# First chunk of x transposed by five DMA transposes, with w1's first slices on ScalarE's queue

## The chip, the cores and the metric

The kernel runs on one core of a Trainium2 chip. The metric is device time in microseconds (us), lower is better. TensorE is written PE in the profile (its weight loads PEld), VectorE DVE, ScalarE ACT, GpSimd POOL and SyncE SP.

## What is computed

The forward and backward pass of a small dense layer, all in bfloat16, with S = 2048 rows of x, D = 640 and F = 1536:

```python
def _fwd_reference(x, w1, w2):          # x [1, S, D], w1 [D, F], w2 [F, D]
    h = jnp.einsum("bsd,df->bsf", x, w1)
    h = jax.nn.silu(h)
    return jnp.einsum("bsf,fd->bsd", h, w2)

def reference(x, w1, w2, grad_out):
    out, vjp = jax.vjp(_fwd_reference, x, w1, w2)
    return (out, *vjp(grad_out))        # out, grad of x, of w1, of w2
```

## The kernel before

The rows of x are worked in four chunks of 512 (`SC`). In each chunk TensorE forms h transposed (F on the partitions, twelve tiles of 128, called `ft`; five steps `dt_` of 128 over D), ScalarE applies silu (`silu_a`, giving aT) and tanh for the derivative (`silu_grad`), then TensorE multiplies aT by w2 for the output (`sd_phase`), forms the gradient of the activation (`g_group`) and multiplies it by w1 transposed for the gradient of x (`sd_phase` again). The activations and their gradients are also stored to scratch in DRAM. After the four chunks the two weight gradients are formed from transposed reloads of that scratch. The h matmuls stand at L206, the gradient ones at L253, those of both `sd_phase` calls at L269, the weight gradients at L357 and L406 (the last tile at L387).

Matmuls contract over the partitions, so x must stand transposed in `xT` (D on the partitions). For chunks 1 to 3 `load_xT` does that with one DMA transpose each (L157). For chunk 0 the kernel loads x plainly in two halves (`x_two`, L173), transposes them on TensorE in twenty 128x128 pieces (L197, with an identity made on GpSimd), and copies the results from PSUM to `xT` on VectorE and ScalarE in turn (L199).

All other transfers are issued by SP, in the order in which they stand in its queue: the two halves of x, the first third of w1 (columns 0 to 511, `FC` = 512) in three pieces by rows (block 0, blocks 1 to `KM`-1, the rest; L178), the second and third thirds of w1 (L169), w2 (L186), then transposes of the first chunk of grad_out (`goT`, L162), of w2 in three pieces (`w2T`, L189) and of w1 (`w1T`, L190).

The start of the kernel has two special parts. 22 matmuls on a constant tile (`NWARM`, L145) keep TensorE at work from the start. And `start_before_entry_wait` moves the instructions listed in `early` (the constant tile's memset, those 22 matmuls, both x loads and the first pieces of w1), with all that stands before them on the same engine, ahead of the wait at which the engines meet on entry.

The first chunk's h is formed by `h_first`: for the first `KM` = 2 blocks of D it goes through four `ft` tiles per block, so that work can begin before all blocks are there; then it completes those four tiles and goes on tile by tile. The tanh of a tile follows its silu by up to `LAG_G` = 4 tiles. The eight PSUM buffers of `ps_h` are shared by all these stages. Transfers are tracked by eight semaphores in turn: the ninth transfer waits until the first has landed, and so on. The order of instructions within an engine is otherwise set by a scheduler.

Of the kernel before, what the change touches and what calls it, by code (L numbers as in the profile page):

```python
# [8 lines left out]

ACT = mybir.ActivationFunctionType  # L10
ALU = mybir.AluOpType
# [4 lines left out]
def start_before_entry_wait(nc, names):  # L16

    def move(nc):
        blocks = nc.m.functions[0].blocks
        entry, home = blocks[0].instructions, blocks[1].instructions
        for engine in {i.engine for i in home if i.name in names}:
            mine = [i for i in home if i.engine == engine]
            last = max(k for k, i in enumerate(mine) if i.name in names)
            moved = mine[: last + 1]
            gate = next(
                k
                for k, i in enumerate(entry)  # L30
                if i.engine == engine and isinstance(i, mybir.InstEventSemaphore)
            )
            taken = {i.name for i in moved}
            for k in reversed(range(len(home))):
                if home[k].name in taken:
                    del home[k]
            for i in reversed(moved):
                entry.insert(gate, i)

    nc.at_finalize(move)  # L40
# [22 lines left out]
def kernel(  # L63
# [11 lines left out]
    nc = tc.nc  # L75
    P = 128
    x2 = x.flatten_outer_dims()
# [5 lines left out]
    S, D = x2.shape  # L83
    F = w1.shape[1]
    ST, DT, FT = S // P, D // P, F // P
    SC = 512
    NCH = S // SC
    STC = SC // P
    FC = 512
# [1 line left out]
    FB = FC // P  # L91
    LAG = 2
    LAG_G = 4
    KM = 2
    NWARM = 22
    dt_in = x.dtype

# [3 lines left out]
    ps_h = ctx.enter_context(tc.tile_pool(name="ps_h", bufs=8, space=bass.MemoryType.PSUM))  # L101
# [10 lines left out]
    w1_v = w1.rearrange("(dt p) f -> p dt f", p=P)  # L112
# [19 lines left out]
    with ExitStack() as mctx:  # L132
        cpool = mctx.enter_context(tc.tile_pool(name="cpool", bufs=1))
# [7 lines left out]
        early = [nc.vector.memset(warm[:], 1.0)]  # L141
# [2 lines left out]
        for i in range(NWARM):  # L144
            early.append(nc.tensor.matmul(wp[:, 0:P], lhsT=warm[:], rhs=warm[:], start=True, stop=True))  # L145

        ident = cpool.tile([P, P], dt_in, name="ident")
        make_identity(nc, ident[:])

        w1_nat = w1pool.tile([P, DT, F], dt_in, name="w1_nat", tag="w1a")  # L150
        w2T = wpool.tile([P, DT, F], dt_in, name="w2T")
        w2_nat = wpool.tile([P, FT, D], dt_in, name="w2_nat")
# [2 lines left out]
        def load_xT(c):  # L155
            xT = xpool.tile([P, DT, SC], dt_in, name="xT")
            nc.sync.dma_start_transpose(out=xT[:], in_=x2[c * SC:(c + 1) * SC, :])  # L157
            return xT
# [4 lines left out]
            return goT  # L163

        xT_next = xpool.tile([P, DT, SC], dt_in, name="xT")
        x_two = cpool.tile([P, 2, 2, D], dt_in, name="x_two")

        def load_w1(lo, hi):
            nc.sync.dma_start(out=w1_nat[:, :, lo:hi], in_=w1_v[:, :, lo:hi])  # L169

        def load_x_half(half):
            lo = half * 2 * P
            return nc.sync.dma_start(  # L173
                out=x_two[:, half, :, :], in_=x2[lo:lo + 2 * P, :].rearrange("(p q) d -> p q d", q=2)
            )

        def load_w1_rows(lo, hi):
            return nc.sync.dma_start(out=w1_nat[:, lo:hi, 0:FC], in_=w1_v[:, lo:hi, 0:FC])  # L178

        early += [load_x_half(0), load_x_half(1), load_w1_rows(0, 1), load_w1_rows(1, KM)]  # L180
        load_w1_rows(KM, DT)
        start_before_entry_wait(nc, {i.ins.name for i in early})
        for fc in range(1, NFC):
            load_w1(fc * FC, (fc + 1) * FC)
# [3 lines left out]
        for fc in range(NFC):  # L188
            nc.sync.dma_start_transpose(out=w2T[:, :, fc * FC:(fc + 1) * FC], in_=w2[fc * FC:(fc + 1) * FC, :])  # L189
        nc.sync.dma_start_transpose(out=w1T[:], in_=w1[:, :])  # L190

        def pe_x_half(xT, half):
            lo = half * 2 * P
            for dt_ in range(DT):
                tp = ps_h.tile([P, 2, P], dt_in, name="tp", tag="hp")
                for q in range(2):
                    nc.tensor.transpose(tp[:, q, :], x_two[:, half, q, dt_ * P:(dt_ + 1) * P], ident[:])  # L197
                copy = nc.scalar.copy if dt_ % 2 else nc.vector.tensor_copy
                copy(out=xT[:, dt_, lo:lo + 2 * P].rearrange("p (s q) -> p q s", q=2), in_=tp[:])  # L199

        pe_x_half(xT_next, 0)
        pe_x_half(xT_next, 1)

        def h_mm(hp, ft, xT, lo, hi):
            for dt_ in range(lo, hi):
                nc.tensor.matmul(  # L206
                    hp[:],
                    lhsT=w1_nat[:, dt_, ft * P:(ft + 1) * P],
                    rhs=xT[:, dt_, :],
                    start=(dt_ == 0),  # L210
                    stop=(dt_ == DT - 1),
                )
# [19 lines left out]
        def h_first(xT, aT, ghT):  # L232
            hps = []
            for ft in range(FB):
                hps.append(ps_h.tile([P, SC], FP32, name="hp"))
            for dt_ in range(KM):
                for ft in range(FB):
                    h_mm(hps[ft], ft, xT, dt_, dt_ + 1)
            for i in range(FT + LAG_G):
                if i < FT:  # L240
                    if i < FB:
                        h_mm(hps[i], i, xT, KM, DT)
                    else:
# [40 lines left out]
        for c in range(NCH):  # L284
            xT, goT = xT_next, goT_next
# [3 lines left out]
            if c + 1 < NCH:  # L289
                xT_next = load_xT(c + 1)  # L290
# [8 lines left out]
            if c == 0:  # L299
                h_first(xT, aT, ghT)  # L300
                nc.sync.dma_start(
                    out=aT_scr[:, c * SC:(c + 1) * SC].rearrange("(ft p) s -> p ft s", p=P), in_=aT[:]
                )
                sd_phase(c, w2_nat, aT, oT_scr)
                for ft in range(FT):
                    g_group(ft, goT, ghT)
                nc.sync.dma_start(
                    out=ghT_scr[:, c * SC:(c + 1) * SC].rearrange("(ft p) s -> p ft s", p=P), in_=ghT[:]
# [4 lines left out]
            for i in range(FT + LAG):  # L313
# [7 lines left out]
                out=aT_scr[:, c * SC:(c + 1) * SC].rearrange("(ft p) s -> p ft s", p=P), in_=aT[:]  # L321
            )
            nc.sync.dma_start(
                out=ghT_scr[:, c * SC:(c + 1) * SC].rearrange("(ft p) s -> p ft s", p=P), in_=ghT[:]
# [7 lines left out]
    with ExitStack() as fctx:  # L332
# [17 lines left out]
        k = 0  # L350
# [26 lines left out]
        k = 0  # L377
        for fc in range(NFC):
            gh_blk = gh_blks[fc]
            for dt_ in range(DT):  # L380
                if dt_ == DT // 2:
                    store_gw2(fc)
                if fc == NFC - 1 and dt_ == DT - 1:
                    for k, (lo, hi) in enumerate(((0, FC - P), (FC - P, FC))):
# [12 lines left out]
                        else:  # L397
                            nc.vector.tensor_copy(out=g1[:, lo:hi], in_=gp[:, lo:hi])  # L398
                        last_store = nc.sync.dma_start(
                            out=gw1_v[:, dt_, fc * FC + lo:fc * FC + hi], in_=g1[:, lo:hi]  # L400
# [49 lines left out]
```

## Time and profile before

| | |
|---|---|
| median of 7 runs | 320.74 us (320.51 to 321.18) |
| profiled execution | 321.41 us, of which the span from first to last instruction is 319.5 us |
| first matmul of the warm-up | starts 0.50 us |
| first h matmuls | from 5.26 us on (in the chain of waits from 5.46) |
| first chunk's output matmuls | from 18.77 us on (in the chain from 18.94) |
| x by halves, 320 KB each | issued 0.09 and 0.54, landed 3.0 and 3.4 us later |
| table load on ScalarE | 0.73 to 2.01 us |
| first silu on ScalarE | 8.40 us |
| goT transpose's issue on SP | 4.75 to 16.0 us |

All times count from the first instruction of the span. The chain of waits is followed back from the last instruction: at each step to what released it, or to the instruction before it on its engine; work in it sets the end, other work does not. A transfer has two times: that for which its issue holds the engine, and that from issue to landing. A row of the timeline gives start, length, engine, line, operation and tiles; "x22" is how many instructions are merged in it. In rows by window, the engines' busy times stand in the order PE, PEld, DVE, ACT, POOL, then the granted clock, the DMA engines' busy share and GB/s.

### The profile page before, as it was taken

How to read it: one execution, taken by the hardware profiler on the slowest of the kernel's cores; microseconds unless marked ns; L12 is line 12 of the kernel's file. 1: busy time of each engine (PE TensorE's matmuls, PEld its weight loads, DVE VectorE, ACT ScalarE, POOL GpSimd, SP SyncE). 2: the span in 40 equal slices, each digit the busy share in tenths (PEclk: the TensorE clock that was granted, in tenths of full speed). 3: DMA queues.
4: the chain of work that ended last, by engine and by line, in shares of the span. 5: the costliest groups of instructions: out<-in, count | busy, mean ns of one | idle time of the engine just before them, and what ended most of it. 6: DMA issues, size and time to landing. Idle time of an engine off the chain costs nothing.

```text
span 319.5 us, 3570 instructions
## 1 busy us (share of the span) xinstructions
PE 316.2 (99%) x1498; PEld 146.3 (46%) x1498; DVE 102.6 (32%) x182; ACT 77.9 (24%) x142; POOL 0.7 (0%) x6
## 2 busy tenths in 40 slices
PE   9999999999999999999999999999999999999996
PEld 6444444444444444444444444444444444444443
DVE  3771541477510087710147741000000100001001
ACT  4960000545201254411054520110100001001100
POOL 0000000000000000000000000000000000000000
PEclk9999999999999999999999999999999999999999
DMA  8999999999999855292635079819999998996011
GB/s 280 322 208 222 215 309 240 342 256 289 277 284 282 207 188 163 84 310 75 161 119 140 2 258 268 216 23 296 261 213 253 261 244 297 235 297 220 33 37 45
DMA packets 147311, 67.33 MB, mean 211 GB/s; under 512 B 112608, under 2 KB 147040, under 8 KB 147296
## 3 DMA queue, kind: packets, MB, share of 16 engines
q1 hardware_dynamic: 147296, 67.12, 80.8%
q8 instruction: 11, 0.18, 0.2%
q14 instruction: 4, 0.03, 0.0%
HBM read 9.83 MB, written 28.97 MB: 121 GB/s over the span
## 4 chain that ended last, share of the span: by engine, by line
PE 98%; DMA 1%; DVE 0%; issue 0%; DVEq 0%; SPq 0%
PE hp L269 32%; PE hp L206 16%; PE hp L253 16%; PE hp L357 16%; PE hp L406 15%; PE hp L387 1%; DMA x_two<-in_x_dram 1%; PE tp L197 1%; DVE g L398 0%; DVEq L398 0%; SPq L434 0%
## 5 line engine op out<-in xcount | busy, mean ns | idle before, releaser
L206 PE MATMUL hp<-xT,w_nat 128*128 128x512 bf16 x240 | 57.4, 382 | 0.0
L253 PE MATMUL hp<-goT,w2T 128*128 128x512 bf16 x240 | 56.9, 379 | 0.0
L269 PE MATMUL hp<-aT,w_nat 128*128 128x512 bf16 x240 | 52.5, 379 | 0.0
L269 PE MATMUL hp<-ghT,w1T 128*128 128x512 bf16 x240 | 52.5, 379 | 0.0
L357 PE MATMUL hp<-a_blk,go_nat 128*128 128x512 bf16 x240 | 52.0, 379 | 0.0
L406 PE MATMUL hp<-gh_blk,x_nat 128*128 128x512 bf16 x224 | 48.5, 379 | 0.0
L277 ACT ACTIVATE oT<-hp 128x512 bf16<-128x512 f32 x24 | 14.3, 597 | 109.8 <-PE hp L269 109.8
L215 ACT ACTIVATE aT<-hp 128x512 bf16<-128x512 f32 x48 | 30.0, 627 | 33.1 <-PE hp L206 33.1
L206 PEld LDWEIGHTS <-w_nat 128*128 128x128 bf16 x240 | 23.7, 99 | 28.5 <-issue 0.8
L357 PEld LDWEIGHTS <-go_nat 128*128 128x128 bf16 x240 | 23.5, 98 | 28.3
L253 PEld LDWEIGHTS <-w2T 128*128 128x128 bf16 x240 | 23.5, 98 | 28.3
L269 PEld LDWEIGHTS <-w1T 128*128 128x128 bf16 x240 | 23.5, 98 | 28.3
L269 PEld LDWEIGHTS <-w_nat 128*128 128x128 bf16 x240 | 23.5, 98 | 28.3
L279 DVE CAST oT<-hp 128x512 bf16<-128x512 f32 x16 | 11.1, 692 | 77.0 <-PE hp L269 77.0
L260 DVE SCALAR_TENSOR_TENSOR ghT<-ghT,hp 128x512 bf16<-128x512 bf16 x48 | 32.5, 682 | 7.3 <-PE hp L253 7.3
L406 PEld LDWEIGHTS <-x_nat 128*128 128x128 bf16 x224 | 21.9, 98 | 26.4
L222 DVE SCALAR_TENSOR_TENSOR ghT<-aT,v 128x512 bf16<-128x512 bf16 x48 | 32.8, 687 | 0.5
L221 DVE TENSOR_SCALAR v<-t 128x512 bf16<-128x512 f32 x48 | 20.3, 426 | 30.6 <-ACT t L219 30.6
L219 ACT ACTIVATE t<-hp 128x512 f32<-128x512 f32 x48 | 29.9, 628 | 0.0
L417 DVE CAST g<-hp 128x512 bf16<-128x512 f32 x7 | 4.8, 692 | 47.0 <-PE hp L406 27.8
L367 DVE CAST g2T<-hp 128x512 bf16<-128x512 f32 x7 | 4.8, 691 | 46.1 <-PE hp L357 46.1
L365 ACT ACTIVATE g2T<-hp 128x512 bf16<-128x512 f32 x8 | 4.8, 597 | 47.0 <-PE hp L357 47.0
(20 smaller groups left out, 27.0 us busy)
## 6 DMA issues: line engine op xcount, KB each, us to landing
aT_scr<-aT SPq DMA_DIRECT2D x4, 1536.0 KB, 6.2
ghT_scr<-ghT SPq DMA_DIRECT2D x4, 1536.0 KB, 8.0
out_dram<-o_sb SPq DMA_DIRECT2D x8, 640.0 KB, 3.6
oT_scr<-oT SPq DMA_DIRECT2D x4, 640.0 KB, 3.6
go_nat<-in_grad_out_dram SPq DMA_DIRECT2D x4, 640.0 KB, 6.6
x_nat<-in_x_dram SPq DMA_DIRECT2D x4, 640.0 KB, 5.4
gxT_scr<-oT SPq DMA_DIRECT2D x4, 640.0 KB, 4.7
w_nat<-in_w_dram SPq DMA_DIRECT2D x1, 1920.0 KB, 12.3
```

Source lines behind the costliest of these rows:

```text
L206: nc.tensor.matmul(hp[:], lhsT=w1_nat[:, dt_, ft * P:(ft + 1) * P], rhs=xT[:, dt_, :], start=(dt_ == 0), stop=(dt_ == DT - 1),)
L215: nc.scalar.activation(aT[:, ft, :], hp[:], ACT.Silu)
L219: nc.scalar.activation(t[:], hp[:], ACT.Tanh, scale=0.5)
L221: nc.vector.tensor_scalar(out=v[:], in0=t[:], scalar1=-0.5, scalar2=0.5, op0=ALU.mult, op1=ALU.add)
L222: nc.vector.scalar_tensor_tensor(out=ghT[:, ft, :], in0=aT[:, ft, :], scalar=1.0, in1=v[:], op0=ALU.subtract, op1=ALU.mult)
L253: nc.tensor.matmul(gp[:], lhsT=w2T[:, dt_, ft * P:(ft + 1) * P], rhs=goT[:, dt_, :], start=(dt_ == 0), stop=(dt_ == DT - 1),)
L260: nc.vector.scalar_tensor_tensor(out=ghT[:, ft, :], in0=ghT[:, ft, :], scalar=1.0, in1=gp[:], op0=ALU.add, op1=ALU.mult)
L269: nc.tensor.matmul(op_[:], lhsT=w_all[:, ft, dt_ * P:(dt_ + 1) * P], rhs=rhs_all[:, ft, :], start=(ft == 0), stop=(ft == FT - 1),)
L277: nc.scalar.activation(oT[:, dt_, :], op_[:], ACT.Copy)
L279: nc.vector.tensor_copy(out=oT[:, dt_, :], in_=op_[:])
L357: nc.tensor.matmul(gp[:], lhsT=go_nat[:, st, dt_ * P:(dt_ + 1) * P], rhs=a_blk[:, st, :], start=(st == 0), stop=(st == ST - 1),)
L406: nc.tensor.matmul(gp[:], lhsT=x_nat[:, st, dt_ * P:(dt_ + 1) * P], rhs=gh_blk[:, st, :], start=(st == 0), stop=(st == ST - 1),)
```

## The change

The first chunk of x is no longer loaded plainly and transposed on TensorE. Five DMA transposes on SP, one for each 128 columns of x (512 rows each), write `xT` directly, ahead of the entry wait. The first third of w1 is loaded by ScalarE's queue, in three pieces (block 0, block 1, blocks 2 to 4), all of them ahead of the entry wait. `KM` becomes 3. The identity, `x_two`, the TensorE transposes and their copies are gone. The other loads keep their place in SP's queue.

```diff
-    KM = 2
+    KM = 3
...
-        ident = cpool.tile([P, P], dt_in, name="ident")
-        make_identity(nc, ident[:])
...
-        x_two = cpool.tile([P, 2, 2, D], dt_in, name="x_two")
...
-        def load_x_half(half):
-            lo = half * 2 * P
-            return nc.sync.dma_start(
-                out=x_two[:, half, :, :], in_=x2[lo:lo + 2 * P, :].rearrange("(p q) d -> p q d", q=2)
-            )
-
         def load_w1_rows(lo, hi):
-            return nc.sync.dma_start(out=w1_nat[:, lo:hi, 0:FC], in_=w1_v[:, lo:hi, 0:FC])
-
-        early += [load_x_half(0), load_x_half(1), load_w1_rows(0, 1), load_w1_rows(1, KM)]
-        load_w1_rows(KM, DT)
+            return nc.scalar.dma_start(out=w1_nat[:, lo:hi, 0:FC], in_=w1_v[:, lo:hi, 0:FC])
+
+        for k in range(DT):
+            early.append(
+                nc.sync.dma_start_transpose(out=xT_next[:, k, :], in_=x2[0:SC, k * P:(k + 1) * P])
+            )
+        early += [load_w1_rows(0, 1), load_w1_rows(1, 2), load_w1_rows(2, DT)]
         start_before_entry_wait(nc, {i.ins.name for i in early})
...
-        def pe_x_half(xT, half):
-            lo = half * 2 * P
-            for dt_ in range(DT):
-                tp = ps_h.tile([P, 2, P], dt_in, name="tp", tag="hp")
-                for q in range(2):
-                    nc.tensor.transpose(tp[:, q, :], x_two[:, half, q, dt_ * P:(dt_ + 1) * P], ident[:])
-                copy = nc.scalar.copy if dt_ % 2 else nc.vector.tensor_copy
-                copy(out=xT[:, dt_, lo:lo + 2 * P].rearrange("p (s q) -> p q s", q=2), in_=tp[:])
-
-        pe_x_half(xT_next, 0)
-        pe_x_half(xT_next, 1)
```

## The prediction

> **What bounds the kernel now.** I read the page first, for the busy shares and the chain; then the chain in order of time; then the timeline of the first 24 us; and last the DMA rows that come nearest to what is added.
>
> ```profile
> span 319.5 us, 3570 instructions
> PE 316.2 (99%) x1498; PEld 146.3 (46%) x1498; DVE 102.6 (32%) x182; ACT 77.9 (24%) x142; POOL 0.7 (0%) x6
> PE 98%; DMA 1%; DVE 0%; issue 0%; DVEq 0%; SPq 0%
> ```
>
> TensorE is busy for 99% of the span and makes 98% of the chain. Only its opening can be shortened: from about 5 us on, no other engine or transfer is in the chain until the last store.
>
> ```profile
> 0.09 3.01 DMA x_two<-in_x_dram
> 3.15 2.31 PE tp L197 x20
> 5.46 13.47 PE hp L206 x60
> 18.94 12.95 PE hp L269 x60
> ```
>
> These rows of the chain in order of time give start, length and work. The first half of x lands at 3.10; twenty transposes run to 5.46; then come the 60 matmuls of the first chunk's h and the 60 of its output. Both groups of 60 are 128x512, yet one takes 13.47 us and the other 12.95 (216 ns each): 0.52 us is lost inside the first group. The timeline shows where:
>
> ```profile
> 0.50 2.53 PE L145 MATMUL wp<-warm 128*128 128x128 bf16 x22 [0.50 <-DVE warm L141]
> 3.15 2.31 PE L197 MATMUL tp<-ident,x_two 128*128 128x128 bf16 x20
> ...
> 5.68 0.15 PEld L206 LDWEIGHTS <-w_nat 128*128 128x128 bf16 x1 [0.28 <-issue]
> 6.11 0.15 PEld L206 LDWEIGHTS <-w_nat 128*128 128x128 bf16 x1 [0.28 <-issue]
> 6.47 11.97 PEld L206 LDWEIGHTS <-w_nat 128*128 128x128 bf16 x56 [0.21 <-issue]
> ```
>
> Weight loads go one per matmul. Until 6.4 they stand 0.43 us apart (5.68 to 6.11); afterwards 11.97/56 = 0.214. So TensorE begins at half rate and doubles it at about 6.4, after 5.9 us of work (from 0.50) with one break of 0.12 us (3.03 to 3.15). Each microsecond at half rate loses 1 - 0.216/0.43 = 0.50 us. The warm-up matmuls and the transposes filled most of that slow time.
>
> ```profile
> 152.55 2.68 SPq L122 DMA_TRANSPOSE o_sb<-oT_scr  x1
> ...
> o_sb<-oT_scr SPq DMA_TRANSPOSE x1, 4.7
> ...
> 12.00:13.00 1.00, 1.00 (x7) 0.44 (x5) 0.97 (x3) 1.00 (x3) 0.00 (x0) 1.00 1.07 364
> 153.80:154.30 0.50, 0.50 (x4) 0.20 (x2) 0.50 (x1) 0.00 (x0) 0.00 (x0) 1.00 0.42 100
> 155.00:156.00 1.00, 1.00 (x6) 0.46 (x5) 0.00 (x0) 0.00 (x0) 0.00 (x0) 1.00 1.26 286
> ```
>
> This is a DMA transpose of 640x512 alone on the queue: 2.68 us of issue, landed 4.7 us after its start. In the window rows the last figure is GB/s: 100 in its first half microsecond of traffic, 286 at its best, against 364 for plain loads (12 to 13 us).
>
> **The change, part by part.** *Removed from the path:* the twenty TensorE transposes (2.31 us), and with them the wait for their ten copies. The copies (six of 0.44 us on VectorE, four of 0.45 on ScalarE) and the identity (0.2 and 0.3 us on GpSimd) lay beside TensorE; their removal is worth nothing by itself.
>
> *Added: when can the first h matmul start?* It needs the first transposed slice and row block 0 of w1. No row shows a 512x128 transpose, so bounds. A slice is a fifth of the instruction above. If the slice comes alone, it lands earlier by the data of four slices: 4 x 131 KB / 286 GB/s = 1.83 us, so 4.7 - 1.83 = 2.9 after its issue at 0.09, at 3.0. If the pieces land no sooner than the whole, 4.8. Now w1 travels at the same time from ScalarE's queue; blocks 0 and 1 (262 KB at 364 GB/s) take 0.72 us. I take 3.0 + 0.7 = 3.7: the low end because five instructions have five completions, plus the traffic beside it. Block 0 of w1 is no later: 128 KB blocks landed 4.2 us after issue with 640 KB of x queued ahead of them, 128 KB stores alone 1.7, and it is now issued near 0.1, so it lands between 1.8 and 4.3. Start at 3.7 instead of 5.46: **-1.76**.
>
> Slices 1 to 4 follow about 0.54 us apart by issue (2.68/5), or 0.86 with all of w1's 1.8 us spread over the four gaps and the last; four h matmuls per slice take 1.7 us at half rate and 0.86 at full rate. None is waited for.
>
> *What goes the other way:* TensorE now has nothing between the last warm-up at about 3.0 and 3.7, and the 2.31 us of transposes no longer use up slow time. If the break does not matter, the rate doubles at 6.4 as now. If it starts the count anew, the doubling comes 5.9 us after 3.7, at 9.6. That is half rate for 2.7 to 5.9 us of h, against 0.94 now. The seven runs say that 5.9 us is on the long side: the profiled execution took 321.41 (its span of 319.5 plus 1.9 around it), 0.67 over the median of 320.74. Read as slow time that is 0.67/0.50 = 1.3 us, so an ordinary run needs about 4.6 us. An ordinary run of before then loses nothing in h and ends it near 18.94 - 0.52 = 18.42. I take the count as starting anew, because 0.7 us of idling is six times the break that the trace shows to be harmless: 4.6 us at half rate, **+2.3**. End of h after: 3.7 + 12.95 + 2.3 = 18.95, or +0.53. In the profiled run's own terms: 3.7 + 12.95 + 0.5 x 5.9 = 19.6 against 18.94, +0.66, which puts it at 322.07; less the 0.67, 321.4. The two ways give 321.3 and 321.4.
>
> The Trainium skill, "TensorE: Matmul & The Clock Gate", Part 1 (the HAM clock gate), speaks against this change: the array runs at half clock until a free-running window of about 3.4 us has been busy. The trace's change from 0.43 to 0.214 us agrees in size. By the page alone a start at 3.7 doubles somewhere from 7.1 to 10.5, and 8.8 in the middle would make the added loss 2.55 and the time 321.6; that the moment differs from run to run is something the single trace here cannot show.
>
> *The rest of the loads.* SP issues five transposes (2.7 to 3.3 us) and only then the second third of w1, before at 2.48; it and what follows also wait for the tracking semaphores of the early transfers (block 0 of w1, then slices 0 and 1, landed by about 4.5). Queued behind are w2, goT and the w2T transposes. The DMA engines stay fed, for 1.3 MB are still ahead. In bytes: the lone transpose shows its first traffic 1.3 us after its issue and lands 0.6 after its last, so from 1.3, x takes 2.3 us at 286 GB/s (3.2 at the 208 of the whole stage from 20 to 25 us), w1's first third 1.8 and its second 1.8; with 0.6 to land, 7.8 to 8.7. The second third is needed after 20 h matmuls, at 12.3 at half rate, at 9.4 if the rate doubles at 6.4. No cost. w2, issued at 3.58 and landed 12.3 later at 15.9, moves by the slower x (655 KB at 208 to 286 instead of 364): 16.4 to 17.2, needed at 18.95. Here the slow h is the cover; without it h would end at 16.65 and wait for w2 by up to 0.6.
>
> The Trainium skill, "Advanced Engine Details and Errata", X-Bar Transpose (TRN2), calls transposes as fast as regular DMAs, 350 to 400 GB/s; the row above has 286 at best. By the page x would cost w2 nothing.
>
> *ScalarE* issues three loads (0.43 each by the rows of SP's w1 loads) ahead of its table load (1.28) and one small activation: ready near 3, its first silu at 9.7. That silu comes after 14 matmuls instead of 11, since KM is 3; it was at 8.40, and the 24 activations behind it run 0.48 apart. The last silu, finished at 19.8 before, moves to about 21.0; the output matmuls want it 11 matmuls after 18.95, at 21.3. Cover of 0.3 us; lost, it costs perhaps 0.5. Later moves in SP's order (the ghT store ahead of a goT load) stand before needs tens of microseconds away.
>
> **Sum:** -1.76 + 2.3 = +0.54 to +0.66; I say 321.4.
>
> **Rivals.** *The break is forgiven* (the other side). The rate doubles where it does now: at 5.1 in an ordinary run, 6.4 at the latest. h ends at 3.7 + 12.95 + 0.7 = 17.35, held back to about 17.6 by w1 and w2, or at 18.0. Against 18.42 that is 319.9 to 320.3. For it: a break of 0.12 us did no harm. Against it: this one is six times longer, and the transposes that kept TensorE at work are gone. It decides if x lands by about 3.3, or if breaks up to 0.9 us are passed over. *The terms cancel:* a half-rate time of only 3.3 to 3.8 us gives 320.6 to 320.9. *x comes late:* transposes that share the DMA engines with w1 land near the upper bound, 4.8. Then h ends at 4.8 + 12.95 + 2.3 = 20.05, which makes 322.4; for it speak the 100 GB/s at which a transpose starts, against it the free queue. That the change does not do what it says I rule out: the program's order has no transpose left on TensorE.
>
> **How the numbers follow.** Forecast 0.45 (own range 320.9 to 322.0), break forgiven 0.27, terms cancel 0.12, x late 0.16. Faster or slower means by over 0.2%, 0.64 us, about what a measurement can tell. Faster: 0.22 of the forgiven and 0.02 of the cancelling case, 0.24. Slower: 0.25 of the forecast and all of x late, 0.41. Same: the rest, 0.35. The range goes from the forgiven case's low end to the late case: 319.8 to 322.5.
>
> **What would show it.** Right: weight loads of the first h 0.43 us apart from about 3.7 to beyond 8, then 0.214, and the chain's 60 h matmuls taking over 15 us. Wrong: a doubling near 6, an idle row of TensorE before 3.5 or after 4.5, or waits within h on w1, w2 or silu.

## The result, and the profile after

The changed kernel takes 322.90 us (median of 12 runs, 322.54 to 324.50) against 320.82 for the kernel before (30 runs): a ratio of 1.0064, 95% interval 1.0053 to 1.0076. It is slower by 2.1 us where 0.7 was forecast, and lies above the range. In the profiled execution the span grew from 319.5 to 321.6, so its 2.1 us can be looked for in the trace. (Both profiled executions lie some 0.5 us above the median of their kernel: 323.36 and 321.41 us.) First the page of the changed kernel: its head, the busy times (share, count), and the chain by engine.

```profile
span 321.6 us, 3522 instructions
PE 316.3 (98%) x1478; PEld 144.6 (45%) x1478; DVE 99.7 (31%) x176; ACT 76.5 (24%) x138; POOL 0.2 (0%) x4
PE 95%; DMA 2%; DVE 0%; issue 0%; DVEq 0%
```

TensorE's busy time is the same although twenty transposes are gone: half-rate matmuls took their place. Transfers now hold 2% of the chain. The chain in order of time (start, length, work):

```profile
6.67 5.54 DMA w_nat<-in_w_dram
12.26 8.81 PE hp L186 x40
21.07 12.95 PE hp L249 x60
```

The first chunk's output begins at 21.07; before, it began at 18.94. The difference of 2.13 us is the whole loss, and from there on the two kernels go alike. What the chain stands on is no longer x but a load of w1: issued at 6.67, landed at 12.22. It is the second third, which the 21st h matmul needs. The timeline of TensorE (matmuls), of its weight loads and of SP, each as start, length, engine, line, operation, and in brackets the idle time before it and what ended that:

```profile
0.08 6.45 SPq L171 DMA_TRANSPOSE xT<-in_x_dram  x5
...
3.70 1.86 PE L186 MATMUL hp<-xT,w_nat 128*128 128x512 bf16 x4 [0.67 <-DMA xT<-in_x_dram]
...
6.49 5.17 PE L186 MATMUL hp<-xT,w_nat 128*128 128x512 bf16 x16 [0.93 <-DMA xT<-in_x_dram]
...
6.67 1.05 SPq L164 DMA_DIRECT2D w_nat<-in_w_dram  x2
...
9.44 0.15 PEld L186 LDWEIGHTS <-w_nat 128*128 128x128 bf16 x1 [0.28 <-issue]
9.77 1.39 PEld L186 LDWEIGHTS <-w_nat 128*128 128x128 bf16 x7 [0.19 <-issue]
...
12.26 8.81 PE L186 MATMUL hp<-xT,w_nat 128*128 128x512 bf16 x40 [0.60 <-DMA w_nat<-in_w_dram]
```

h starts at 3.70, to the digit as forecast. But after four matmuls TensorE waits for the second slice of x until 6.49, and after twenty for w1 until 12.26. The rate doubles near 9.7: weight loads 0.43 us apart up to 9.44, 0.2 from 9.77 on. SP's two rows tell why the later wait, for w1, exists: five transposes hold SP from 0.08 to 6.53, and the second third of w1 is issued only then. Why the second slice came late is a question for the experiments. What one transpose costs shows in the rows of tile `xT` (issue time on SP as minimum, median, maximum in ns; then from issue to landing in us):

```profile
L171 SPq DMA_TRANSPOSE xT<-in_x_dram x5: 1242/1261/1262, 0.1 to 5.3; - x5
DMA to landing us min/median/max: 3.1/3.8/5.1
```

An issue takes 1.26 us. The prediction had 0.54. Nor do the DMA engines stay fed. Here is a low stretch, a row by window, whose last figure is GB/s; a load of 640 KB had been issued at 6.67:

```profile
7.50:8.50 1.00, 1.00 (x4) 0.29 (x2) 0.00 (x0) 0.00 (x0) 0.00 (x0) 1.00 0.37 67
```

Added up along TensorE, h ends at 3.70 + 15.84 of matmuls (1.86, 5.17 and 8.81) + 0.93 and 0.60 of waits = 21.07. The second path lies close under the first: the first twenty matmuls ended at 11.66, so with w1 there in time h would have ended only 0.60 us sooner.

### The profile page after: what moved, and what is told of

Read it like the earlier page. It is cut to its first block, busy times and chain, and to the rows that moved or that the text cites. A ratio compares the mean times of both kernels' runs of the same rounds, so it can differ in the third digit from the quotient of the medians.

```text
span 321.6 us, 3522 instructions
## 1 busy us (share of the span) xinstructions
PE 316.3 (98%) x1478; PEld 144.6 (45%) x1478; DVE 99.7 (31%) x176; ACT 76.5 (24%) x138; POOL 0.2 (0%) x4
## 4 chain that ended last, share of the span: by engine, by line
PE 95%; DMA 2%; DVE 0%; issue 0%; DVEq 0%
PE hp L249 32%; PE hp L337 16%; PE hp L233 16%; PE hp L386 15%; PE hp L186 15%; DMA w_nat<-in_w_dram 2%; PE hp L367 1%; DVE g L378 0%; DVEq L378 0%
## 5 line engine op out<-in xcount | busy, mean ns | idle before, releaser
L186 PE MATMUL hp<-xT,w_nat 128*128 128x512 bf16 x240 | 59.6, 391 | 2.2 <-DMA xT<-in_x_dram 1.6
L195 ACT ACTIVATE aT<-hp 128x512 bf16<-128x512 f32 x48 | 28.7, 605 | 37.7 <-PE hp L186 37.6
L199 ACT ACTIVATE t<-hp 128x512 f32<-128x512 f32 x48 | 28.6, 605 | 0.0
```

Of the source, the lines that this page charges most:

```text
L186: nc.tensor.matmul(hp[:], lhsT=w1_nat[:, dt_, ft * P:(ft + 1) * P], rhs=xT[:, dt_, :], start=(dt_ == 0), stop=(dt_ == DT - 1),)
L195: nc.scalar.activation(aT[:, ft, :], hp[:], ACT.Silu)
L199: nc.scalar.activation(t[:], hp[:], ACT.Tanh, scale=0.5)
```

## The experiments

Theory A was that the issue time of the five transposes, by way of the late load of w1, sets the end of h; theory B that the half rate does, as predicted; theory C that loads on a second queue slow the transposes. Each kernel was timed beside the kernel before on its own chip, so kernels of different groups are best compared by their ratios. `KM` = 3 was not tried alone.

**More warm-up matmuls** (e3): is the half rate what was lost?

```diff
-    NWARM = 22
+    NWARM = 31
```

> 31 warm-up matmuls instead of 22, which reach to the start of h at 3.7; all else as in the changed kernel. Theory B: with the break gone the rate doubles earlier and some 2 us come back, 320.9. Theory A: the matmuls of the first 20 may run faster, but the 21st still waits for the second third of w1 at 12.2, so nothing changes: 322.9, within 0.3.

Measured: 322.69 us, ratio 1.0084 (1.0051 to 1.0118); four of seven runs at 322.2 to 322.7, three at 324.8 to 325.5, which no profile here explains. By the median that is 0.2 us less than the changed kernel; the ratio is higher than its 1.0064 because of the three long runs. The matmuls of TensorE in its profile:

```profile
0.52 3.49 PE L144 MATMUL wp<-warm 128*128 128x128 bf16 x31 [0.52 <-DVE warm L140]
...
6.43 3.61 PE L186 MATMUL hp<-xT,w_nat 128*128 128x512 bf16 x15 [1.32 <-DMA xT<-in_x_dram]
11.39 8.81 PE L186 MATMUL hp<-xT,w_nat 128*128 128x512 bf16 x40 [1.34 <-DMA w_nat<-in_w_dram]
```

All but the first few of the first twenty h matmuls now run at full rate; they end 1.6 us sooner (6.43 + 3.61 = 10.04 instead of 6.49 + 5.17 = 11.66), and TensorE then waits longer for the same load. The half rate was real but lay under that wait. Theory B falls as the sole cause of the loss: without the half rate most of it is still there. But it lay only 0.60 us under the wait, and the landing itself moves by more than that: issued at 6.67 and 6.65, the load landed at 12.22 in the profile of the changed kernel and at 11.34 in this one. The edit does not explain that difference, and it makes the 0.9 us between the two spans (321.6 and 320.7). In an ordinary execution the two bounds may be about level.

**The second and third thirds of w1 on ScalarE's queue** (e1): does it help to take them from behind the transposes?

```diff
         def load_w1(lo, hi):
-            nc.sync.dma_start(out=w1_nat[:, :, lo:hi], in_=w1_v[:, :, lo:hi])
+            nc.scalar.dma_start(out=w1_nat[:, :, lo:hi], in_=w1_v[:, :, lo:hi])
```

> The second and third thirds of w1 go to ScalarE's queue, behind the first third; all else is as in the changed kernel. Theory A (the five transposes hold SP for 6.3 us, so the second third of w1 is issued at 6.67 and lands at 12.22, and that sets the end of h): the second third lands by about 9, the 20 first h matmuls still end near 11.3 because of the slices and the half rate, h ends near 11.3 + 8.65 = 19.95 instead of 21.07, and the time falls by 1.1 us to about 321.8. Theory B (the half rate after the break decides, as predicted): the first 20 matmuls are untouched, no change, 322.9.

Measured: 324.73 us, ratio 1.0118 (1.0089 to 1.0146): slower still, against both theories. The chain in order of time, and then the rows of `xT`:

```profile
2.65 7.94 DMA xT<-in_x_dram
10.64 3.53 PE hp L186 x9
```

```profile
L171 SPq DMA_TRANSPOSE xT<-in_x_dram x5: 1235/1261/1293, 0.1 to 5.3; - x5
DMA to landing us min/median/max: 3.7/6.3/7.9
```

The load was issued early, at 2.70, but the third slice of x, issued at 2.65, now landed 7.94 us later. The issue on SP took no longer: what suffered is the transfer. That gave theory C its weight.

**Blocks 2 to 4 of w1's first third behind the transposes** (e8): theory C by itself.

```diff
-        early += [load_w1_rows(0, 1), load_w1_rows(1, 2), load_w1_rows(2, DT)]
+        early += [load_w1_rows(0, 1), load_w1_rows(1, 2)]
         start_before_entry_wait(nc, {i.ins.name for i in early})
+        nc.sync.dma_start(out=w1_nat[:, 2:DT, 0:FC], in_=w1_v[:, 2:DT, 0:FC])
```

> Blocks 2 to 4 of w1's first third (384 KB) are no longer loaded by ScalarE at 1.1 but by SP behind the five transposes; blocks 0 and 1 stay where they are. Theory C: the second slice of x lands near 4.3 instead of 6.45 and the others 1.25 us apart behind it, since nothing competes after 3. Theory D (a transpose starts only when the one before has landed): the second slice lands near 5.5 to 6.5 all the same. The matmuls then wait for blocks 2 to 4 near 10 and for the second third of w1 near 13, so the time is 323.5 to 324.5 either way.

Measured: 325.83 us, ratio 1.0154 (1.0128 to 1.0180), above the 323.5 to 324.5 expected; TensorE stood 3.3 us for blocks 2 to 4. But the rows of `xT` decide between C and D:

```profile
L171 SPq DMA_TRANSPOSE xT<-in_x_dram x5: 1240/1261/1262, 0.1 to 5.3; - x5
DMA to landing us min/median/max: 2.8/2.8/3.7
```

With nothing on the other queue after blocks 0 and 1, a slice lands 2.8 us after its issue instead of 3.8 in the median and 5.1 at worst. The second slice landed at 4.22 instead of 6.45, and TensorE went from the first slice to it without a wait. So the 384 KB on ScalarE's queue cost it 2.2 us. It landed 0.4 us after the first slice (3.83), so a transpose does not wait for the one before it. After the wait of 3.3 us the matmuls ran at half rate until 13.5, which goes with the time above the expectation. The issue stays at 1.26, with or without company.

**w1's first third on SP ahead of the transposes** (e4), no load on ScalarE at all:

```diff
-            return nc.scalar.dma_start(out=w1_nat[:, lo:hi, 0:FC], in_=w1_v[:, lo:hi, 0:FC])
+            return nc.sync.dma_start(out=w1_nat[:, lo:hi, 0:FC], in_=w1_v[:, lo:hi, 0:FC])
...
+        early += [load_w1_rows(0, 1), load_w1_rows(1, 2), load_w1_rows(2, DT)]
         for k in range(DT):
             early.append(
                 nc.sync.dma_start_transpose(out=xT_next[:, k, :], in_=x2[0:SC, k * P:(k + 1) * P])
             )
-        early += [load_w1_rows(0, 1), load_w1_rows(1, 2), load_w1_rows(2, DT)]
```

> The three pieces of w1's first third go back to SP's queue, ahead of the five transposes; no transfer is issued by ScalarE. Theory C (a transfer on the other queue slows the transposes: the second slice landed 5.1 us after its issue, the first 3.6): each slice lands 2.4 to 3 us after its issue, and the issues shorten to about 0.55 us. Theory A: an issue still takes 1.26 us, the whole is shifted by three issues of 0.43, the second third of w1 lands near 13.5, and the time rises by 1.3 us to about 324.2; the slices may still land sooner after their issue.

Measured: 323.91 us, ratio 1.0095 (1.0079 to 1.0111). The issues took 1.20 to 1.26 each, so that part of C's expectation fails and A's holds. The slices landed 4.7 us after their issue at first and 2.8 at last, so C's 2.4 to 3 us fails for all but the last ones. The first landed at 6.16, behind the 640 KB of w1 in its own queue. TensorE's row of the timeline (one of the 60 records is missing):

```profile
6.20 15.91 PE L186 MATMUL hp<-xT,w_nat 128*128 128x512 bf16 x59 [3.16 <-DMA xT<-in_x_dram]
```

h ran from 6.20 to 22.11 almost without a wait; 0.43 us from matmul to matmul until 11.9. Here the half rate had no cover: 60 matmuls took 15.9 us instead of 12.95.

**One transpose in place of five** (e2):

```diff
-        for k in range(DT):
-            early.append(
-                nc.sync.dma_start_transpose(out=xT_next[:, k, :], in_=x2[0:SC, k * P:(k + 1) * P])
-            )
+        early.append(nc.sync.dma_start_transpose(out=xT_next[:], in_=x2[0:SC, :]))
```

> One DMA transpose of all 640 columns in place of five of 128; all else as in the changed kernel. Theory A: its issue takes about 3.3 us instead of 6.3, the second third of w1 is issued near 3.4 and lands near 9; x lands whole at 4.8 to 5.5, so h starts later but without stalls between slices, partly at half rate: end of h 19.7 to 20.4 against 21.07, time 321.5 to 322.2. Theory B: TensorE's break grows from 0.7 to over 2 us, so the time is 322.9 or more.

Measured: 324.91 us, ratio 1.0123 (1.0104 to 1.0142). The issue did fall to 3.16, and the second third of w1 landed at 9.57. But the chain shows x itself:

```profile
0.09 7.82 DMA xT<-in_x_dram
7.95 2.29 PE hp L183 x5
```

It landed 7.82 us after its issue instead of the 4.7 of the lone transpose of that size (640x512) in the kernel before, with w1's first third on the other queue. h could not start before 7.95.

**The second third of w1 in two halves** (e6), and the same with 31 warm-up matmuls (e7): is the late load the bound, and what comes next?

```diff
-        for fc in range(1, NFC):
-            load_w1(fc * FC, (fc + 1) * FC)
+        load_w1(FC, FC + FC // 2)
+        load_w1(FC + FC // 2, 2 * FC)
+        load_w1(2 * FC, 3 * FC)
```

> The second third of w1 is loaded in two halves of 256 columns, one after the other on SP; all else as in the changed kernel. Theory A (the landing of that load sets the end of h): the first half lands near 11 instead of 12.2, the 21st matmul no longer waits or by less, h ends 0.7 to 1.1 us sooner, time 321.8 to 322.2. If the landing is not the bound: 322.9, unchanged.

> As the split load, with 31 warm-up matmuls instead of 22. 31 alone changed nothing (322.69) because the wait for w1 covered the half rate. With the wait shortened the cover is smaller: if the half rate is the next bound, this is 0.3 to 0.9 us faster than the split load alone, 321.0 to 321.6; if not, the two are equal.

Measured: 322.45 us, ratio 1.0044 (1.0024 to 1.0064), and 321.65 us, ratio 1.0026 (1.0008 to 1.0044). The first half landed at 10.1 to 10.4. With 22 warm-ups the 21st matmul found it there. TensorE's row:

```profile
6.18 14.27 PE L187 MATMUL hp<-xT,w_nat 128*128 128x512 bf16 x55 [0.61 <-DMA xT<-in_x_dram]
```

The second slice of x and then the remaining matmuls in a row, at half rate until about 10.3, set the end of h at 20.45: 0.62 us sooner than in the changed kernel, a little less than the 0.7 to 1.1 expected. With 31, which alone had gained 0.2 by the median, the median fell by another 0.8 us, though the intervals overlap. That fits two costs one behind the other: the half rate shows once the wait for w1 is short. The chain of the second kernel names a third bound:

```profile
8.35 11.73 DMA w_nat<-in_w_dram
20.12 1.90 PE hp L250 x8
```

That is w2, issued at 8.35 behind everything else and landed at 20.07; before the change it was there at 15.9. TensorE stood 0.84 us for it. But this execution took 322.58 us, 0.93 above the median of its kernel, so that the median run waits for w2 is not shown.

**Two transposes, w1's blocks 2 to 4 between them** (e9), and with 22 warm-ups (e10). These put together what the others showed: fewer issues, less company on the other queue, no idle TensorE.

```diff
-    KM = 3
-    NWARM = 22
+    KM = 2
+    NWARM = 31
...
+        early.append(x_cols(0, 2))
+        early.append(nc.sync.dma_start(out=w1_nat[:, 2:DT, 0:FC], in_=w1_v[:, 2:DT, 0:FC]))
+        early.append(x_cols(2, DT))
+        early += [load_w1_rows(0, 1), load_w1_rows(1, 2)]
```

(`x_cols(lo, hi)` is one DMA transpose of those blocks of 128 columns on SP; the five transposes and the third piece on ScalarE are gone.)

> Two DMA transposes (256 and 384 columns) in place of five; blocks 2 to 4 of w1's first third go on SP between the two, blocks 0 and 1 stay on ScalarE's queue; KM is 2, and 31 warm-up matmuls reach to the start of h. If an issue costs a fixed 0.79 us plus 0.475 per 128 columns (from 1.26 for one and 3.16 for five), the two issues take 1.73 and 2.21, the second third of w1 is issued near 4.6 instead of 6.67 and lands at 8.5 to 9.5; x and w1's first third are there by 6.5 to 7. Then the end of h is 18.0 to 19.5 and the time 320.3 to 321.7: 1.2 to 2.6 us faster than the changed kernel and about level with the kernel before. If the cost is per column, the issues take 2.5 and 3.8 and the time stays at 322 or above.

> The same with 22 warm-up matmuls, so that TensorE idles from 3.0 to the start of h. With the waits for slices and w1 mostly gone, the half rate has no cover left: 0.8 to 2.3 us slower than with 31 (theory B in its place). If the waits are still the bound, the two are equal within 0.3.

Measured: 321.38 us, ratio 1.0018 (1.0007 to 1.0028), and 321.83 us, ratio 1.0028 (1.0015 to 1.0042). SP's rows of the first:

```profile
0.09 1.33 SPq L170 DMA_TRANSPOSE xT<-in_x_dram  x1
1.48 0.57 SPq L175 DMA_DIRECT2D w_nat<-in_w_dram  x1
2.10 1.63 SPq L170 DMA_TRANSPOSE xT<-in_x_dram  x1
3.86 2.34 SPq L164 DMA_DIRECT2D w_nat<-in_w_dram  x2
```

SP is through with x at 3.73 instead of 6.53, the second third of w1 lands at 9.90 instead of 12.22 and w2 at 17.2 instead of 19.4, and 1.5 of the 2.1 us come back. Neither cost model that was expected fits: 256 columns took 1.33 and 384 took 1.63 (1.93 in e10). With 1.26 for 128 and 3.16 for 640, all but the 1.63 lie near 0.63 us per 128 columns with a floor near 1.25, and not a fixed sum on top. What is left in the chain is the wait for the second part of x, which landed at 7.75 (`DMA xT<-in_x_dram` from 2.10, 5.66 us). Without the longer warm-up the median is 0.45 us higher, less than the 0.8 expected, and the intervals overlap. Its chain is bound by the half rate:

```profile
4.54 14.97 PE hp L190 x60
```

No version that was tried is faster than the kernel before.

**Only w1's first third on ScalarE's queue** (e5): the other part of the change alone, in the kernel before.

```diff
-            return nc.sync.dma_start(out=w1_nat[:, lo:hi, 0:FC], in_=w1_v[:, lo:hi, 0:FC])
+            return nc.scalar.dma_start(out=w1_nat[:, lo:hi, 0:FC], in_=w1_v[:, lo:hi, 0:FC])
...
-        early += [load_x_half(0), load_x_half(1), load_w1_rows(0, 1), load_w1_rows(1, KM)]
-        load_w1_rows(KM, DT)
+        early += [load_x_half(0), load_x_half(1), load_w1_rows(0, 1), load_w1_rows(1, KM), load_w1_rows(KM, DT)]
```

> The kernel before with one part of the change alone: the three pieces of w1's first third go to ScalarE's queue ahead of the entry wait; x still comes by halves and TensorE transposes, KM stays 2. If a load on the other queue only saves SP's issue time: the second third of w1 is issued at 1.1 instead of 2.48, h starts no later than 5.46, time 320.8, within 0.3. If the two queues slow each other (theory C): x lands later than 3.1 and 3.9, by up to the 0.7 us of w1's first two blocks, and the time rises to 321.2 to 321.8.

Measured: 323.21 us, ratio 1.0065 (1.0047 to 1.0082), as much as the whole change and more than either expectation. Its chain, and then TensorE's rows of the timeline:

```profile
1.11 7.95 DMA w_nat<-in_w_dram
9.11 1.90 PE hp L205 x8
```

```profile
5.41 1.67 PE L205 MATMUL hp<-xT,w_nat 128*128 128x512 bf16 x7
9.11 11.40 PE L205 MATMUL hp<-xT,w_nat 128*128 128x512 bf16 x51 [2.02 <-DMA w_nat<-in_w_dram]
```

x was hardly later (4.40 for the second half against 3.95). But blocks 2 to 4 landed at 9.07 instead of 6.75: SP, relieved, issued the second third of w1 at 1.08, just ahead of them (1.11), and it landed at 8.73. Two loads under way together, one needed at once and one later, is the reading that fits; on one queue they had landed in order (6.75 and 8.61). In the changed kernel this is not at work, for there the second third is issued at 6.67, after blocks 2 to 4 have landed (6.23): that both kernels lose about 2 us is chance.

**Blocks 0 and 1 alone on ScalarE's queue** (e11):

```diff
         def load_w1_rows(lo, hi):
-            return nc.sync.dma_start(out=w1_nat[:, lo:hi, 0:FC], in_=w1_v[:, lo:hi, 0:FC])
+            eng = nc.scalar if hi <= KM else nc.sync
+            return eng.dma_start(out=w1_nat[:, lo:hi, 0:FC], in_=w1_v[:, lo:hi, 0:FC])
```

> The kernel before with only blocks 0 and 1 of w1's first third (256 KB) on ScalarE's queue; blocks 2 to 4 go on SP ahead of the second third, as before. With all three pieces on ScalarE's queue it took 323.21, and TensorE stood from 7.1 to 9.1 for blocks 2 to 4. If the loss came from the order (the second third, on the other queue, overtook blocks 2 to 4), it vanishes: blocks 2 to 4 land by 7, time 320.8, within 0.3. If any load on the second queue costs time by slowing x, h starts later than 5.46 and the time stays above 321.5.

Measured: 322.60 us, ratio 1.0043 (1.0021 to 1.0065), but from 320.95 to 323.92. In the profiled run, the fastest (320.95), blocks 2 to 4 landed at 6.61, as when all went on SP, and the 2 us wait was gone; the second half of x landed at 4.67 instead of 3.95. So the order explains e5's wait, as far as one profile shows. But the median is not the 320.8 that this would give; what makes the other runs of this kernel slower is not in that profile and stays open.

## Why the prediction was wrong

- *The start of h* (3.7 instead of 5.46, -1.76): right; it started at 3.70. Both terms of it fit: without other traffic a slice landed 2.8 us after its issue (e8, against 2.9), and the first slice, beside blocks 0 and 1 of w1, after 3.6, each time about 0.2 us after block 1 (3.47 and 3.66 here; the same in e1, e3, e6, e7 and e8).
- *"Slices 1 to 4 follow about 0.54 us apart by issue (2.68/5)"*, and with it *"SP issues five transposes (2.7 to 3.3 us)"*: this is the step that failed. An issue took 1.26 us, the five 6.45. The nearest row was an instruction that read 640 rows by 512 columns, so four blocks of 128 source columns; by blocks it said 0.67. And to divide it at all assumed that a part of the work costs that part of the time; the floor of about 1.25 cannot be seen in a row of long instructions. What the step is worth: with two issues (e9) 1.5 of the 2.1 us come back, and 1.1 with the warm-up as it was (e10), each together with the other edits in it.
- *"The DMA engines stay fed"*: wrong; 67 GB/s from 7.5 to 8.5, with the second third of w1 issued at 6.67.
- *The second third of w1*, 7.8 to 8.7, *"No cost"*: it landed at 12.22, 3.5 us beyond the upper figure, and was issued 3.4 us later than the upper figure for that (6.67 against 3.3). TensorE stood 0.60 us for it, and it set the end of h: 12.26 + 8.81 = 21.07, where 18.95 to 19.6 was predicted.
- *"None is waited for"* (slices 1 to 4): wrong, by the traffic. The second slice landed at 6.45 and was waited for 0.93 us; e8 puts 2.2 us of its delay on the 384 KB on ScalarE's queue, and without them, at the same issue times, it was not waited for. The prediction let w1's traffic delay only the first slice, and spread the rest by bytes.
- *The half rate* (+2.3, doubling 4.6 to 5.9 us after the start): the mechanism is there, doubling near 9.7, 6 us after 3.70. In the profiled run's own terms the prediction had 3.7 + 12.95 + 2.95 = 19.6 for the end of h. The matmuls took 15.84 us against those 15.90, so the whole miss in that sum is the two waits, 0.93 + 0.60, which it put at nothing. That the length fits so well is partly luck: the wait of 0.93 lies inside it, and in e6, with the same start, the doubling came only at about 10.3. Nor would removing the half rate have helped much by itself: it lay under the wait for w1 (e3), seems to cost about 0.8 us once that wait is shorter (e6 and e7), and cost 3 us in e4, where nothing hid it. The forecast named a right effect and missed the bound above it.
- *w2 at 16.4 to 17.2*: 19.4 in fact, by the same issue time; harmless here, in the chain of e7's profile.
- *ScalarE*: ready at 3.2 against "near 3" was right; the first silu came at 10.40 instead of 9.7, with the matmuls before it. The rival in which x comes late had the right sign and 322.4, but by a late first slice.
- Of the signs, one of each kind came: weight loads 0.43 us apart to beyond 8, and waits within h on w1.
- Two figures do not follow from their own terms: 0.54 + 1.8/5 is 0.90 and not 0.86, and the middle case by the page comes to 321.5 and not 321.6. Nothing rests on either.
- e5 shows besides that the second queue, costed only as a delay of x, loses 2 us by itself in the kernel before.

## What to carry to other kernels

Cost an issue by rows of its own size: a short DMA transpose held its queue nearly as long as one of twice the columns (1.26 and 1.33 us), and everything behind it moves by the sum. A second queue removes order as well as issue time, so look at which load is needed first and what will now run beside it. And before pricing a slow stretch of TensorE, ask which wait would cover it.

## What the runs showed of the hardware

The issue of a DMA transpose of 512 rows took 1.26 us for 128 columns, 1.33 for 256, 1.6 to 1.9 for 384 and 3.16 for 640. With nothing else under way on the other queue, a 512x128 transpose landed 2.8 us after its issue (e8). With a plain load there it took up to 5.1 (384 KB) or 7.9 us (384 and 640 KB, e1), though 384 KB are only about 1.1 us at the 364 GB/s of the plain loads before. In five kernels the second slice landed just behind the 384 KB, by 0.2 to 0.3 us (6.23 and 6.45 in the changed kernel; also e1, e3, e6, e7).

The moment at which TensorE's rate doubled is not fixed. From the end of the last wait before it, it came after 2.9 us in e1 and e2, 3.3 in the changed kernel and e8, about 4 in e6 and e10 and 5.7 in e4. With the same 22 warm-up matmuls from 0.5 on, it came at 6.4 in the profile before, but in those of e5 and e11 all h matmuls, from 5.4 and 5.5 on, ran at full rate. Once doubled, the rate stayed so over waits of 1.34 us (e3) and 2.02 us (e5). The granted clock of the profile does not tell the two rates apart: it is 1.00 in the window row above, at half rate.

The Trainium skill, "DMA: Bandwidth & Descriptors", Rules for kernel authors, says that spreading transfers over issuing engines adds no bandwidth and only saves issue time. e5 agrees that issue time was saved (the second third of w1 issued at 1.08 instead of 2.48), and adds that it can cost 2 us. "TensorE: Matmul & The Clock Gate", Part 1, has a free-running window of about 3.4 us; an estimate from it puts the doubling 3.4 to 6.8 us after a resume. The 4 and 5.7 us above lie in that, the 3.3 at its edge, and the 2.9 of e1 and e2 do not.
